# One core: the order of all work taken from a list scheduler over five engines, and the high part of each weight block rounded on GpSimd

## The chip, the cores and the metric

One core of a Trainium2 chip runs the kernel. The metric is the time of one execution in microseconds (us) on the device, the median of several runs. Five engines work side by side, each through its own queue in order: TensorE (PE, with its weight loads PEld), VectorE (DVE), ScalarE (ACT), GpSimd (POOL) and SyncE (SP), which here only issues DMA transfers. PSUM, where matmuls put their results, has eight banks of 128x512 fp32.

## The reference

```python
def phi(x):                       # x scaled by 64**-0.25
    h = einsum('bhsd,md->bhsm', x, omega) - sum(x * x, -1) / 2
    return exp(h - max(h, -1)) / sqrt(m)
q_p, k_p = phi(q_s), phi(k_s)     # 8 batches, 8 heads, 576 positions, 128 features
kv  = einsum('bhsm,bhsd->bhmd', k_p, v)
z   = sum(k_p, axis=2)
out = einsum('bhsm,bhmd->bhsd', q_p, kv) / (einsum('bhsm,bhm->bhs', q_p, z) + 1e-6)
x   = out as 4608 tokens x 512
h   = x @ w_in                    # 512 x 2048, float64 weights
result = (h * sigmoid(h)) @ w_out # 2048 x 512, float64 weights
```

## The kernel before

The attention is done in 32 windows, one for each pair of heads of a batch; four windows give the 512 channels of one batch's tokens. A window n goes through a chain over all engines. SP loads its transposed rows (`rawk`, `rawq`), its natural rows (`nat`) and `vt`. PE projects k and q (L136, eight matmuls into two banks) and the ninth, mixed chunk (L181, "mid", one bank). DVE takes the maxima (L159, L187) and forms the shift `nb` (L152, L153); for the first eight windows (`DIRECT`) ACT applies the exponential straight from the bank (L167, L191), later DVE subtracts (L171, L193) and ACT does one exponential over the tile (L199). POOL adds up k's features (L209 to L214), PE spreads the sum to all rows (L220), ACT copies it (`zb`), DVE forms the denominators (L265 to L269), POOL divides (L272), PE transposes q's nine chunks in three groups (L283), ACT copies each (L284), PE multiplies with the turned kv (L293), and ACT and DVE split the result into a high and a low part (`xh`, `xl`, L304, L305).

The MLP runs in 9 x 16 = 144 steps (t, f): t is a block of 512 tokens (the ninth holds the last 64 tokens of each batch), f a block of 128 of the 2048 columns. All operands are split in a high and a low fp32r part, so that a step has 12 matmuls of stage 1 (L409) into a bank `ph`, two Silu activations on ACT (L413, L414), a subtraction on DVE (`gl`, L415), and, two steps later (`LAG`), 12 matmuls of stage 2 (L425) into the four accumulators `po`. Two banks serve `ph`, so stage 1 of step i+2 needs `gl` of step i to be done. The weights come as float64. A block of 128x512 is put together from its words: ACT L371, DVE L372, L373 and L376, then ACT rounds the high part (L377) and POOL subtracts (L378). There are 32 blocks, all prepared during the first 16 steps; those of `w_out` also go to DRAM (`wo_d`) and are read again for t > 0.

The order is written by hand: each piece of work is put into one list with a key (`POS` and `PPOS` give a window's keys, 8 units are one step, a window takes 32) and the list is sorted by key; the framework then lays the instructions out, engine by engine. Windows 0 to 3 and parts of window 4 come before the first step. From step 2 on attention has two banks (`ps_a`), in turn; before that it uses up to eight.

Of the kernel before, what the change touches and what calls it, by code (L numbers as in the profile page):

```python
# [18 lines left out]
P = 128  # L19
# [32 lines left out]
PPOS = {
    "loadk": 1, "loadq": 1.1, "loadv": 1.2, "sqk": 6, "sqq": 6.1,
    "z": 0, "kv": 1, "zcopy": 1.2, "den": 2.2, "norm": 5, "kvturn": 2,
    "projk": 0.1, "evack": 0.3, "midk": 0.2, "mevack": 0.4, "turn": 12.2,
    "projq": 0.5, "evacq": 6, "midq": 0.6, "mevacq": 6.1, "expk": 1.5, "expq": 8, "sums": 9,
    "num": 14,
}
# [3 lines left out]
def attention_mlp(ctx: ExitStack, tc: tile.TileContext, qT, kT, qn, kn, v, om_in, w_in, w_out, out):  # L62
# [4 lines left out]
    xs = ctx.enter_context(tc.tile_pool(name="xs", bufs=2))  # L67
    mlp = ctx.enter_context(tc.tile_pool(name="mlp", bufs=2))
    att = ctx.enter_context(tc.tile_pool(name="att", bufs=1))
    dram = ctx.enter_context(tc.tile_pool(name="dram", bufs=1, space=DRAM))  # L70
    ps_acc = ctx.enter_context(tc.tile_pool(name="ps_acc", bufs=4, space=PSUM))
    ps_h = ctx.enter_context(tc.tile_pool(name="ps_h", bufs=2, space=PSUM))
    ps_att = ctx.enter_context(tc.tile_pool(name="ps_att", bufs=2, space=PSUM))
# [6 lines left out]
    oms = const.tile([P, M], F32, tag="oms", name="oms")  # L80

    def warm(count):
        ps = ps_att.tile([P, 512], F32, tag="att", name="ps_warm")
        for _ in range(count):
            nc.tensor.matmul(ps[:, :P], ones, ones, start=True, stop=True)

    wide = [8]
    rr = [0]

    def bank():  # L90
        if wide[0]:
            rr[0] += 1
            i = rr[0] % wide[0]
            if i < 4:
                return ps_acc.tile([P, 512], F32, tag="acc", name="ps_w")
            if i >= 6:
                return ps_h.tile([P, 512], F32, tag="h", name="ps_w2")
        return ps_att.tile([P, 512], F32, tag="att", name="ps_a")

    raws, nats, sqs, hs, mxs, nbs, banks, mids, vts = {}, {}, {}, {}, {}, {}, {}, {}, {}  # L100
# [4 lines left out]
    def load(n, who):  # L105
        b, p = divmod(n, NPAIR)
        srcT, srcn = (kT, kn) if who == "k" else (qT, qn)
        raw = att.tile([P, S + P], F32, tag=f"raw{who}", name=f"raw{who}", bufs=2)
        nc.sync.dma_start(raw, srcT[b, p])
        if n == 0 and who == "k":  # L110
            nc.scalar.dma_start(omr, om_in)
        nat = att.tile([P, NC, D], F32, tag="nat", name="nat", bufs=2)
        nc.sync.dma_start(nat, srcn[b, p])
        raws[n, who], nats[n, who] = raw, nat

    def load_v(n):
        b, p = divmod(n, NPAIR)
        vt = att.tile([P, NC + 1, D], F32, tag="v", name="vt", bufs=2)
        nc.sync.dma_start(vt, v[b, p])
        vts[n] = vt  # L120

    def squares(n, who):
        nat = nats.pop((n, who))
        nc.scalar.activation(nat, nat, AF.Square, scale=SCALE * 0.5**0.5)  # L124
        s = att.tile([P, 10], F32, tag=f"sq{who}", name="sq", bufs=2)
        nc.vector.tensor_reduce(s[:, :NC], nat, AX.X, ALU.add)
        sqs[n, who] = s

    def project(n, who):
        raw = raws[n, who]  # L130
        pair = [bank(), bank()]
# [7 lines left out]
        banks[n, who] = pair
        hs[n, who] = att.tile([P, NC, M], F32, tag=f"h{who}", name=f"h{who}", bufs=2)  # L140
        mxs[n, who] = att.tile([P, 10], F32, tag=f"mx{who}", name="mx")
        nbs[n, who] = att.tile([P, 10], F32, tag=f"nb{who}", name="nb")
# [7 lines left out]
    def shift(n, who, part):  # L150
        m, s, nb = part(mxs[n, who]), part(sqs[n, who]), part(nbs[n, who])
        nc.vector.tensor_tensor(nb, m, s, ALU.subtract)  # L152
        nc.vector.scalar_tensor_tensor(nb, nb, -1.0, s, ALU.mult, ALU.subtract)  # L153

    def evacuate(n, who):
        h, m, nb = hs[n, who], mxs[n, who], nbs[n, who]
        pair = banks.pop((n, who))
        for j in range(2):
            nc.vector.tensor_reduce(  # L159
                m[:, 5 * j : 5 * j + 4], pair[j].rearrange("p (c m) -> p c m", m=M), AX.X, ALU.max  # L160
            )
        shift(n, who, sides)
        for j in range(2):
            if n < DIRECT:
                for i in range(4):
                    c = 5 * j + i
                    nc.scalar.activation(  # L167
                        h[:, c], pair[j][:, i * M : (i + 1) * M], AF.Exp, bias=nb[:, c : c + 1]
                    )
                continue  # L170
            nc.vector.tensor_tensor(  # L171
                h[:, 5 * j : 5 * j + 4],
                pair[j].rearrange("p (c m) -> p c m", m=M),
                nb[:, 5 * j : 5 * j + 4].unsqueeze(2).broadcast_to([P, 4, M]),
                ALU.add,
            )

    def project_mid(n, who):
        raw = raws.pop((n, who))
        ps = bank()  # L180
        nc.tensor.matmul(ps[:, :M], raw[:, S:], oms, start=True, stop=True)  # L181
        mids[n, who] = ps

    def evacuate_mid(n, who):
        h, m, nb = hs[n, who], mxs.pop((n, who)), nbs[n, who]
        ps = mids.pop((n, who))
        nc.vector.tensor_reduce(m[:, 4:5], ps[:, :M], AX.X, ALU.max)  # L187
        mxs[n, who] = m
        shift(n, who, middle)
        if n < DIRECT:  # L190
            nc.scalar.activation(h[:, MID], ps[:, :M], AF.Exp, bias=nb[:, 4:5])  # L191
        else:
            nc.vector.tensor_scalar(h[:, MID], ps[:, :M], nb[:, 4:5], None, ALU.add)  # L193
        del mxs[n, who], nbs[n, who], sqs[n, who]

    def expo(n, who):
        if n < DIRECT:
            return
        nc.scalar.activation(hs[n, who], hs[n, who], AF.Exp)  # L199

    ess, zbs, kvs, ens, kts = {}, {}, {}, {}, {}
# [46 lines left out]
    def kv_alone(n):  # L248
        kv(n)
        kt_copy(n)  # L250
# [285 lines left out]
```

## Time and profile before

| | |
|---|---|
| runs | 1109.34 us median of 3 (1109.12 to 1111.86) |
| profiled execution | 1111.65 us, span of the core 1109.8 us |
| busy share of the span | PE 96%, PEld 76%, ACT 53%, DVE 50%, POOL 21% |
| granted TensorE clock | 0.977 of full speed over the span |
| HBM | 138.48 MB read, 19.92 MB written, 143 GB/s |

The span is the time from the first to the last instruction; the execution's own time is 1.85 us longer. A busy share is an average over stages that have different limits: the first 80 us are attention alone, steps 0 to 15 do attention, MLP and the preparation of weights together, steps 16 to about 112 attention and MLP, and the rest the MLP alone.

### The profile page before, as it was taken

The page shows a single profiled execution, that of the slowest core. Times are in us where ns is not written, and L with a number is a line of the kernel's source. Part 1 is how long each engine was busy: PE and PEld are TensorE (multiplying, and loading weights), DVE is VectorE, ACT ScalarE, POOL GpSimd, SP SyncE. Part 2 cuts the span into 40 slices and gives each one's busy share as a digit, 9 for nine tenths or more (in the row PEclk, how much of TensorE's full clock was granted, in tenths as well). Part 3 has the DMA queues.
Part 4 walks back from the last instruction along what each step waited for, and adds up shares of the span by engine and source line. Part 5 has one row for each costly group of instructions (what it writes and reads, how often), then busy time and mean ns, then how long its engine had stood idle before and what let it go on. Part 6 is the DMA issues. An engine that isn't in the chain of part 4 may idle for free.

```text
span 1109.8 us, 16167 instructions
## 1 busy us (share of the span) xinstructions
PE 1066.0 (96%) x5900; PEld 841.2 (76%) x5900; DVE 558.6 (50%) x1125; ACT 584.2 (53%) x1105; POOL 229.5 (21%) x295
## 2 busy tenths in 40 slices
PE   7679898999999999999999999999999999999998
PEld 6447676777778777777777777777777788888886
DVE  6887987745555555455554555455544431111111
ACT  6759677565555555655556555655555542112221
POOL 3544544411111111111111111111111110000000
PEclk7769999999999999999999999999999999999999
DMA  7556666454444344444345444434343226233322
GB/s 264 173 169 213 228 207 226 166 167 128 131 131 162 112 136 138 145 145 132 126 130 164 138 138 128 164 126 135 116 139 113 69 79 203 98 103 118 116 95 76
DMA packets 64223, 159.46 MB, mean 144 GB/s; under 512 B 15376, under 2 KB 15504, under 8 KB 64144
## 3 DMA queue, kind: packets, MB, share of 16 engines
q1 hardware_dynamic: 63680, 157.84, 44.1%
q8 instruction: 47, 0.77, 0.3%
q10 hardware_dynamic: 464, 0.59, 0.2%
q14 instruction: 32, 0.26, 0.1%
HBM read 138.48 MB, written 19.92 MB: 143 GB/s over the span
## 4 chain that ended last, share of the span: by engine, by line
PE 80%; DVE 7%; ACT 6%; issue 2%; POOL 2%; DMA 2%; SPq 0%; ACTq 0%; DVEq 0%; POOLq 0%
PE ph L409 32%; PE po L425 31%; PE ps_a L136 6%; PE ps_a L283 3%; PE ps_a L238 2%; PE ps_a L293 2%; DMA out<-ot 1%; PE ps_a L220 1%; PE ps_a L181 1%; DVE prod L265 1%; ACT L413 1%; ACT L199 1%; DVE w L373 1%; DVE mx L159 1%; DVE w L372 1%
## 5 line engine op out<-in xcount | busy, mean ns | idle before, releaser
L425 PE MATMUL po<-wo,gh 128*128 128x512 f32 x1152 | 379.3, 406 | 0.0
L413 ACT ACTIVATE gh<-ph 128x512 fp32r<-128x512 f32 x144 | 86.2, 599 | 329.2 <-PE ph L409 328.6
L415 DVE TENSOR_TENSOR gl<-ph,gh 128x512 fp32r<-128x512 f32 x144 | 99.0, 687 | 283.1 <-ACT ph L414 283.1
L425 PEld LDWEIGHTS po<-wo,gh 128*128 128x128 f32 x1152 | 205.5, 188 | 40.3 <-ACT hk L167 0.4
L409 PE MATMUL ph<-xh,wh 128*128 128x512 f32 x576 | 233.7, 406 | 0.0
L409 PE MATMUL ph<-xl,wh 128*128 128x512 f32 x576 | 226.7, 394 | 0.0
L409 PE MATMUL ph<-xh,wl 128*128 128x512 f32 x576 | 226.4, 393 | 0.0
L425 PE MATMUL po<-wo,gl 128*128 128x512 f32 x576 | 226.1, 393 | 0.0
L272 POOL TENSOR_TENSOR hq<-hq,rd 128x384 f32<-128x384 f32 x96 | 81.4, 877 | 404.1 <-DVE rd L269 352.8
L159 DVE TENSOR_REDUCE mx<-ps_a 128x4 f32<-128x512 f32 x112 | 73.1, 686 | 119.9 <-PE ps_a L136 119.2
L409 PEld LDWEIGHTS ph<-xh,wh 128*128 128x128 f32 x576 | 108.4, 188 | 26.0 <-issue 1.6
L409 PEld LDWEIGHTS ph<-xh,wl 128*128 128x128 f32 x576 | 108.6, 188 | 23.4
L409 PEld LDWEIGHTS ph<-xl,wh 128*128 128x128 f32 x576 | 108.6, 189 | 23.3
L425 PEld LDWEIGHTS po<-wo,gl 128*128 128x128 f32 x576 | 108.2, 188 | 22.4
L413 ACT ACT_TABLE_LOAD x54 | 69.3, 1283 | 40.1 <-PE ph L409 39.4
L209 POOL TENSOR_TENSOR t<-hk 128x256 f32<-128x256 f32 x64 | 46.2, 737 | 210.6 <-ACT hk L199 180.1
L414 ACT ACTIVATE ph<-ph 128x512 f32<-128x512 f32 x144 | 85.4, 593 | 0.0
L199 ACT ACT_TABLE_LOAD x47 | 60.3, 1283 | 33.8 <-DVE hq L193 33.4
L265 DVE TENSOR_TENSOR prod<-hq,zb 128x512 f32<-128x512 f32 (+1 forms) x96 | 49.0, 563 | 35.0 <-ACT zb L229 34.9
L283 PE MATMUL ps_a<-ident,hq 128*128 128x128 f32 x258 | 43.4, 281 | 10.9 <-ACT hk L191 6.6
L124 ACT ACTIVATE nat<-nat 128x576 f32<-128x576 f32 x64 | 44.8, 702 | 15.1 <-DMA nat<-kn 12.5
L283 PEld LDWEIGHTS ps_a<-ident,hq 128*128 128x128 f32 x258 | 31.1, 142 | 26.8 <-issue 7.6
(96 smaller groups left out, 1190.0 us busy)
## 6 DMA issues: line engine op xcount, KB each, us to landing
wo<-wo_d SPq DMA_DIRECT2D x128, 512.0 KB, 3.4
rawk<-kT SPq DMA_DIRECT2D x32, 352.0 KB, 3.0
rawq<-qT SPq DMA_DIRECT2D x32, 352.0 KB, 3.0
vt<-v SPq DMA_DIRECT2D x32, 320.0 KB, 3.0
nat<-kn SPq DMA_DIRECT2D x32, 288.0 KB, 3.0
nat<-qn SPq DMA_DIRECT2D x32, 288.0 KB, 3.1
wraw<-w_in SPq DMA_DIRECT2D x16, 512.0 KB, 3.9
wraw<-w_out SPq DMA_DIRECT2D x16, 512.0 KB, 4.3
```

Of the source, the lines that this page charges most:

```text
L136: nc.tensor.matmul(pair[j][:, i * M : (i + 1) * M], raw[r, o : o + P], oms[r], start=True, stop=True)
L159: nc.vector.tensor_reduce(m[:, 5 * j : 5 * j + 4], pair[j].rearrange("p (c m) -> p c m", m=M), AX.X, ALU.max)
L199: nc.scalar.activation(hs[n, who], hs[n, who], AF.Exp)
L209: nc.gpsimd.tensor_tensor(t[:, j], e[:, 5 * j : 5 * j + 2], e[:, 5 * j + 2 : 5 * j + 4], ALU.add)
L265: nc.vector.tensor_tensor(prod[:, c, :M], e[:, c], zb[:, j].unsqueeze(1).broadcast_to([P, hi - lo, M]), ALU.mult)
L272: nc.gpsimd.tensor_tensor(e[:, c], e[:, c], rd[:, c].unsqueeze(2).broadcast_to([P, 3, M]), ALU.mult)
L283: nc.tensor.transpose(ps[:, i * P : (i + 1) * P], e[:, 3 * g + i], ident)
L409: nc.tensor.matmul(ph, w[:, k, :], x, start=k == 0 and n == 0, stop=k == NK - 1 and n == 2)
L413: nc.scalar.activation(gh, ph, AF.Silu)
L414: nc.scalar.activation(ph, ph, AF.Silu)
L415: nc.vector.tensor_tensor(gl, ph, gh.bitcast(F32), ALU.subtract)
L425: nc.tensor.matmul(accs[t][j], g[:, js], w, start=f == 0 and n == 0, stop=f == NF - 1 and n == 2)
```

## The change

Every piece of work becomes a unit of a plan, with its engine, a duration written in by hand, a key, what it must follow, and which buffers it takes and frees. A loop takes, over and over, the unit that can start first (with keys deciding within 0.25 us) and so makes one list, in which the units are then recorded. The framework lays out the instructions from that list. Four more things change. The high part of a weight block is rounded by POOL in place of ACT. The word buffer `w32` has three slots in place of two. A block of `w_out` is read back from DRAM at t = 0 as well (16 more reads), through a ring of three in place of four. In windows 0 to 3 the shift is formed in one piece, and x is split in 512+64 columns in place of 288+288.

```diff
+RINGS = {
+    "acc": 4, "h": 2, "att": 2,
...
+    "en": 2, "den": 2, "rd": 2, "wraw": 3, "w32": 3, "wre": 2, "wo": 3, "wp": 2, "gh": 3, "gl": 3, "ot": 2,
+}
+START_MLP = 62.0
+STEP = 7.56
+SLOW = 8.2
+PRO = 11.0
+SWITCH = 1.3
+STAY = 8.0
+HANDOFF = {"PE": 0.3, "ACT": 0.15, "DVE": 0.15, "POOL": 0.2, "SP": 0.2}
+CALM = 0.5
...
+                p = min((p for p in pick if p[3] <= least + 0.25), key=lambda p: p[2:])
+                if best is None or p[3] < best[3]:
+                    best = p
...
+            free_at[e] = t + dur
...
-        nc.scalar.copy(hi, w)
-        nc.gpsimd.tensor_tensor(lo, w, hi.bitcast(F32), ALU.subtract)
...
+    def weight_high(i):
+        nc.gpsimd.tensor_copy(parts_of(i)[0], T["w", i])
+
+    def weight_low(i):
+        hi, lo = parts_of(i)
+        nc.gpsimd.tensor_tensor(lo, T["w", i], hi.bitcast(F32), ALU.subtract)
+
+    def keep_weight(f):
+        nc.sync.dma_start(wo_d[f].bitcast(F32), T.pop(("wp", f)).bitcast(F32))
+
+    def get_weight(t, f):
+        T["wo", t, f] = wo = new("wo", [P, 2, DMODEL], F32R)
+        nc.sync.dma_start(wo.bitcast(F32), wo_d[f].bitcast(F32))
...
+        add(("wh",) + i, "POOL", 0.9, key - 1, lambda: weight_high(i), after=[("wd",) + i + (2,)], alloc=list(more))
+        add(("wlo",) + i, "POOL", 1.05, key, lambda: weight_low(i), after=[("wh",) + i], free=[("w32",) + i])
...
-    for _, f in sorted(queue, key=lambda e: e[0]):
-        f()
+    for u in plan.run():
+        u["fn"](*[bank(p) for p in u["pools"]])
```

The number of instructions stays nearly the same: PE has the same matmuls (eight 64x512 and eight 64x64 products take the place of sixteen 64x288), DVE 1111 rows with its two branches counted against 1127, POOL 32 CASTs more, ACT 32 CASTs fewer and 120 table loads against 108, SP 16 loads of `wo` more.

The first place is PE's queue in steps 6 and 7, where the transposes of window 5 (L283, now L381) meet the mixed chunk of window 6's k (L181, now L269); L409 and L495 are stage 1, L425 and L513 stage 2. Before:

```order
L425 MATMUL po_1100<-wo,gh 128x512
L181 MATMUL ps_a<-oms,rawk 128x128
L425 MATMUL po_1100<-wo,gh 128x512
L425 MATMUL po_1100<-wo,gl 128x512
L425 MATMUL po_1101<-wo,gh 128x512 x2
L283 MATMUL ps_a<-ident,hq 128x128 x3
L425 MATMUL po_1101<-wo,gl 128x512
L409 MATMUL ph<-xh_346,wh_1203 128x512
L283 MATMUL ps_a<-ident,hq 128x128 x6
```

Now:

```order
L381 MATMUL ps_att<-ident,hq 128x128 x3
L495 MATMUL ps_h<-xh_730,wh_1172 128x512
L495 MATMUL ps_h<-xl_731,wh_1172 128x512
L495 MATMUL ps_h<-xh_730,wl_1173 128x512
L269 MATMUL ps_att<-oms,rawk 128x128
L495 MATMUL ps_h<-xh_954,wh_1172 128x512
L381 MATMUL ps_att<-ident,hq 128x128 x3
L495 MATMUL ps_h<-xl_955,wh_1172 128x512
L495 MATMUL ps_h<-xh_954,wl_1173 128x512
L513 MATMUL ps_acc<-wo,gh 128x512 x2
L513 MATMUL ps_acc<-wo,gl 128x512
L381 MATMUL ps_att<-ident,hq 128x128 x3
```

The three groups of transposes are spread out, the mixed chunk stands behind the first of them, and the group that takes the mixed chunk's bank (the second before, the third now) is still only six MLP matmuls and one group away from it.

The second place is DVE's queue around the maximum of that same mixed chunk (L187, now L276), with the word operations of weight blocks (L372, L373, L376; now L456, L458, L462) and the shift (L152, L153; now L282, L283). Before:

```order
L373 SCALAR_TENSOR_TENSOR w32_1351<-wre_1352,w32_1351 128x512
L372 TENSOR_SCALAR w32_1377<-wraw_1375 128x512
L376 SCALAR_TENSOR_TENSOR w32_1351<-wraw_1349,w32_1351 128x512
L373 SCALAR_TENSOR_TENSOR w32_1377<-wre_1378,w32_1377 128x512
L376 SCALAR_TENSOR_TENSOR w32_1377<-wraw_1375,w32_1377 128x512
L187 TENSOR_REDUCE mx_1307<-ps_a_1346 128x1
L152 TENSOR_TENSOR nb_1308<-mx_1307,sq_1032 128x1
L153 SCALAR_TENSOR_TENSOR nb_1308<-nb_1308,sq_1032 128x1
```

Now:

```order
L458 SCALAR_TENSOR_TENSOR w32_1409<-wre_1418,w32_1409 128x512
L276 TENSOR_REDUCE mxk_1342<-ps_att_1415 128x1
L462 SCALAR_TENSOR_TENSOR w32_1409<-wraw_1329,w32_1409 128x512
L282 TENSOR_TENSOR nbk_1343<-mxk_1342,sqk_907 128x1
L458 SCALAR_TENSOR_TENSOR w32_1463<-wre_1477,w32_1463 128x512
L283 SCALAR_TENSOR_TENSOR nbk_1343<-nbk_1343,sqk_907 128x1
```

Before, the word operations stand ahead of the maximum; now two of them stand between the maximum and the shift's two halves.

The third place is POOL's queue at the fourth and fifth weight blocks (L378 before; L476 and L480 now), between the sums of k (L209 to L214, now L318 to L323) and the division (L272, now L375). Before:

```order
L378 TENSOR_TENSOR wl_802<-w_805,wh_801 128x512
L378 TENSOR_TENSOR wo<-w_846,wo 128x512
L209 TENSOR_TENSOR t<-hk 128x256 x2
L211 TENSOR_TENSOR es<-t 128x256
L214 TENSOR_TENSOR es<-es,hk 64x128 x2
L272 TENSOR_TENSOR hq<-hq,rd 128x384 x3
```

Now:

```order
L476 CAST wh_759<-w_693 128x512
L480 TENSOR_TENSOR wl_760<-w_693,wh_759 128x512
L476 CAST wp<-w_552 128x512
L318 TENSOR_TENSOR t<-hk 128x256
L480 TENSOR_TENSOR wp<-w_552,wp 128x512
L318 TENSOR_TENSOR t<-hk 128x256
L320 TENSOR_TENSOR es<-t 128x256
L476 CAST wh_939<-w_914 128x512
L480 TENSOR_TENSOR wl_940<-w_914,wh_939 128x512
L323 TENSOR_TENSOR es<-es,hk 64x128 x2
L375 TENSOR_TENSOR hq<-hq,rd 128x384 x3
```

Each block now has two instructions on POOL, and they stand between those of the attention.

## Rows read from the trace of the kernel before

**Rows 1.** Busy time by engine in stretches of the span, TensorE's granted clock, DMA.
```profile
core 0: us, PE busy (x) PEld busy (x) DVE busy (x) ACT busy (x) POOL busy (x), PEclk, DMA share, GB/s
97.50:198.40 100.90, 87.68 (x467) 66.83 (x467) 83.69 (x141) 75.29 (x162) 47.12 (x42) 0.97 0.63 210
198.40:247.60 49.20, 47.44 (x281) 36.96 (x279) 29.30 (x62) 29.94 (x50) 12.60 (x16) 1.00 0.55 176
247.60:1099.00 851.40, 849.30 (x4665) 677.67 (x4664) 368.42 (x765) 409.60 (x698) 122.53 (x179) 1.00 0.40 127
```
**Rows 2.** Timeline of PE: first matmul of steps 3 and 14; the kernel's last.
```profile
97.51 0.50 PE L409 MATMUL ph<-xh,wh 128*128 128x512 f32 x1
...
198.37 0.39 PE L409 MATMUL ph<-xh,wh 128*128 128x512 f32 x1
...
1104.98 0.39 PE L425 MATMUL po<-wo,gl 128*128 128x512 f32 x1
```
**Rows 3.** Who PE waited for, 97.5 to 198.4: total us, times, longest.
```profile
PE ps_a L283 <- ACT hk L191: 6.6, 2, 3.4
PE ps_a L220 <- DVE xl L305: 2.7, 2, 1.3
PE ps_a L181 <- ACT hk L167: 2.2, 2, 2.0
PE ps_a L181 <- ACT hq L167: 1.7, 1, 1.7
```
**Rows 4.** The same view from 198.4 to the end.
```profile
PE ps_a L220 <- DVE xl L305: 2.9, 4, 1.3
```
**Rows 5.** Timeline of DVE, ACT and PE at one of the waits of rows 3.
```profile
128.76 1.22 DVE L373 SCALAR_TENSOR_TENSOR w<-wre,w 128x512 uint32<-128x512 uint32 x1
130.01 1.09 DVE L376 SCALAR_TENSOR_TENSOR w<-wraw,w 128x512 uint32<-128x512 uint32 x1
131.03 0.28 DVE L187 TENSOR_REDUCE mx<-ps_a 128x1 f32<-128x128 f32 x1
...
132.47 0.37 ACT L191 ACTIVATE hk<-ps_a,nb 128x128 f32<-128x128 f32 x1 [2.92 <-DVE nb L153]
...
132.98 0.78 PE L283 MATMUL ps_a<-ident,hq 128*128 128x128 f32 x5 [3.24 <-ACT hk L191]
```
**Rows 6.** Stretches up to the ends of gl of steps 1 and 12, as rows 1.
```profile
0.00:91.40 91.40, 69.14 (x431) 50.43 (x432) 71.96 (x150) 61.81 (x178) 43.24 (x54) 0.76 0.64 204
0.00:193.30 193.30, 157.81 (x909) 117.48 (x910) 154.28 (x287) 140.59 (x349) 91.40 (x97) 0.87 0.64 210
```
**Rows 7.** DVE by line, 0 to 193.3: busy us, mean ns, idle before.
```profile
L376 DVE SCALAR_TENSOR_TENSOR w<-wraw,w 128x512 uint32<-128x512 uint32 x29 | 23.4, 818 | 0.1
L372 DVE TENSOR_SCALAR w<-wraw 128x512 uint32<-128x512 uint32 x30 | 23.0, 775 | 12.8 <-POOL wo L378 7.7 <-POOL wl L378 5.1
L373 DVE SCALAR_TENSOR_TENSOR w<-wre,w 128x512 uint32<-128x512 uint32 x29 | 21.4, 747 | 0.2
L152 DVE TENSOR_TENSOR nb<-mx,sq 128x8 f32<-128x8 f32 x16 | 6.8, 424 | 0.0
```
**Rows 8.** Single lines of DVE over the whole span: duration ns, min/median/max.
```profile
L372 DVE TENSOR_SCALAR w<-wraw x32: 413/462/1568, 27.0 to 199.7; 128x512 uint32<-128x512 uint32 x32
L376 DVE SCALAR_TENSOR_TENSOR w<-wraw,w x32: 673/683/1533, 32.6 to 203.4; 128x512 uint32<-128x512 uint32 x32
L152 DVE TENSOR_TENSOR nb<-mx,sq x128: 142/160/1259, 8.7 to 893.3; 128x8 f32<-128x8 f32 x64, 128x1 f32<-128x1 f32 x64
```
**Rows 9.** POOL by line, 0 to 193.3, as rows 7.
```profile
L378 POOL TENSOR_TENSOR wl<-w,wh 128x512 fp32r<-128x512 f32 x16 | 21.5, 1342 | 9.3 <-ACT wh L377 8.9
L272 POOL TENSOR_TENSOR hq<-hq,rd 128x384 f32<-128x384 f32 x21 | 21.0, 1025 | 15.4 <-DVE rd L269 14.0 <-DVE nb L153 0.9 <-DVE nb L152 0.4
L203 POOL MEMSET prod<- 128x1161 f32 x1 | 1.1, 1072 | 0.0
```
**Rows 10.** ACT by line, 0 to 193.3, as rows 7: one group.
```profile
L413 ACT ACT_TABLE_LOAD x7 | 9.0, 1283 | 0.1
```
**Rows 11.** DMA issues of the weights read again: KB each, us to landing.
```profile
wo<-wo_d SPq DMA_DIRECT2D x128, 512.0 KB, 3.4
```

More of the change, by code (lines that the diff above doesn't have):

```diff
@@ L103, in omega @@
         nc.scalar.mul(oms, omr, SCALE)
[L105 to L114, printed above, removed]
@@ L116, in load_v @@
-    def load_v(n):
[L117 to L123, printed above, removed]
-        nc.scalar.activation(nat, nat, AF.Square, scale=SCALE * 0.5**0.5)
[L125 to L131, printed above, removed]
+    T = {}
@@ L139, in project @@
[L139 to L142, printed above, removed]
+                nc.tensor.matmul(ps[:, i * M : (i + 1) * M], raw[r, o : o + P], oms[r], start=True, stop=True)
+        T["p", n, who, 0], T["p", n, who, 1] = a, b
+        T["h", n, who] = new(f"h{who}", [P, NC, M])
+        T["mx", n, who] = new(f"mx{who}", [P, 10])
@@ L144, in sides, with shift, every @@
+    def shift(n, who, part):
+        m, s, nb = (part(T[a, n, who]) for a in ("mx", "sq", "nb"))
+        nc.vector.tensor_tensor(nb, m, s, ALU.subtract)
+        nc.vector.scalar_tensor_tensor(nb, nb, -1.0, s, ALU.mult, ALU.subtract)
+    def every(a):
+        return a[:, :NC]
     def sides(a):
@@ L148, in middle @@
         return a[:, 4:5]
[L150 to L192, printed above, removed]
+    def expo(n, who, j):
+        h, nb, ps = T["h", n, who], T["nb", n, who], T.pop(("p", n, who, j))
+        for i in range(1 if j == 2 else 4):
+            c = 4 if j == 2 else 5 * j + i
+            nc.scalar.activation(h[:, c], ps[:, i * M : (i + 1) * M], AF.Exp, bias=nb[:, c : c + 1])
@@ L463, in attention_mlp, with at, bk @@
-    for n in range(LEAD, NWIN):
-        queue += window(n, POS, SPACE * (n - LEAD))
-    for f in range(NF):
-        put(8 * (f - AHEAD_IN) + 4.5, weights_in, f)
-    for i in range(NF * (B + 1)):
-        put(8 * (i - AHEAD_OUT) + 3.5, weights_out, *divmod(i, NF))
+    plan = Plan()
+    add = plan.add
+    def at(n, off, steady):
+        if n < LEAD:
+            return PRO * n + off
+        return clock(4 * (n - LEAD - 1) + steady / 8)
+    def bk(name, j=0):
+        return ("bank", name, j)
@@ new lines, in attention_mlp @@
+    last = None
+    for f in range(NF):
+        key = clock(f)
+        weight(("in", f), key - 4, w_in[f], last)
+        last = ("in", f)
+        weight(("out", f), clock(f + LAG) - 3, w_out[f], last,
+               more=[("wp", ("wp", f))])
+        last = ("out", f)
+        add(("keep", f), "SP", 0.42, clock(f + LAG) + 4, lambda f=f: keep_weight(f), after=[("wlo", "out", f)], lat=2.1,
+            free=[("wp", f)])
+    steps = [(t, f) for t in range(B + 1) for f in range(NF)]
+    total = len(steps)
```

703 lines of the change are left out of this document (461 added, 242 removed).

## The prediction

> **What bounds the kernel now.** I read the stretches first, since the busy shares of the whole span average over stages. From 247.6 us to 1099 TensorE works 849.3 of 851.4 us at clock 1.00 [rows 1]: nothing that another engine does there can move the end, and the change leaves PE the same matmuls. So the end moves only by what is gained or lost ahead of about step 20. From step 3 to step 14, 97.5 to 198.4, PE is busy 87.68 of 100.90 us, so 13.2 are idle at clock 0.97 [rows 1]. From there to 247.6 only 1.8 us are idle [rows 1].
>
> Next, who PE waited for. Between 97.5 and 198.4 the four entries sum to 13.2 us, all of the idle time, and every one is a wait for a bank of attention (`ps_a`): 6.6 for the transposes, whose bank still holds k's mixed chunk that ACT has not read; 2.7 for the sum of k (L220), whose bank's last content DVE has not yet split; 3.9 for the mixed chunk's matmul [rows 3]. After 198.4 L220 waits another 2.9 [rows 4]. The timeline shows the costliest wait from inside: the maximum of the mixed chunk starts on DVE at 131.03 behind word operations of 1.22 and 1.09 us, ACT's exponential at 132.47 waited 2.92 us for DVE, and the transposes start at 132.98 after 3.24 us of idle PE [rows 5].
>
> Last, DVE, the engine behind those waits, and its neighbour POOL. Up to 193.3, the end of step 12's `gl` on which step 14 depends, DVE is busy 154.28 us and so idle 39.0 [rows 6]; step 14's first matmul stands at 198.37, 5.1 later [rows 2]. DVE's busy time holds more than the operations need: L372 takes 413 ns at its shortest and 1568 at its longest [rows 8], 775 in the mean up to 193.3 [rows 7].
>
> **The change, part by part.** *The order.* The same count of matmuls stands ahead of steps 3, 8, 14 and 20 in both orders (283, 446, 658, 879; now 878), so no work is moved across these places on PE, and what counts is when the banks come free. Three terms.
>
> (a) Up to step 3. It starts at 97.51 [rows 2], and needs `gl` of step 1, which ends at 91.4 with DVE busy 71.96 us and idle 19.4 [rows 6]. The new order has 153 DVE instructions ahead of that `gl` where 148 were: the words of twelve weight blocks in place of eight, and fewer attention pieces. The words of four blocks at their minima, 0.41 + 0.67 + 0.67 each, are 7.0 [rows 8] with L373 taken as L376; the rest of the exchange I put at 2, by counting, and the locks (below) at 2. So DVE is busy 83. Before, the idle 19.4 were mostly waits for transfers and banks; with more work at hand I take 14 to be left. 83 + 14 = 97 for `gl` would be 5 late; but the `gl` of step 1 no longer stands as far ahead of step 3's place on PE, where 283 matmuls must be done in either order by then at the same clock. I take 0, with bounds of -5 (the idle time shrinks by 5 more) and +5.4 (all of it shows).
>
> (b) Steps 3 to 14. The wait of L220 goes: PE work between the last user of its bank and L220 was 2.6 us and is 5.7 to 6.9 in the new order, against a longest wait of 1.3 [rows 3]: -2.7. The transposes wait little less. In the second place of the order the distance from the mixed chunk to the group that takes its bank is 1.9 to 2.5 us of PE work where it was 1.6 to 1.9, and of DVE's chain the word operations that stood ahead of the maximum now stand between it and the two halves of the shift: the chain is no shorter by them. On ACT the mixed chunk's exponential stands between the Silu activations of a step in some windows, which costs table loads of 1.28 us [rows 10]. I take -2.0 of 6.6. The mixed chunk's matmul has less distance than before in one of its two kinds (6.6 and 5.6 us, against 9.5 and 5.7): 3.9 stay. Sum -4.7; bounds -13.2 (all idle time gone) and 0.
>
> (c) After step 14. L220's distance rises from 2.6 to 3.3 or 4.0 us; its four waits average 0.7 [rows 4]: -2.5 of 2.9.
>
> *The cast on POOL.* On ACT it frees 32 instructions, but ACT is idle 53 us of 193 [rows 6] and is waited for only through DVE [rows 5], so the gain there is nothing beyond (b), and twelve more table loads of 1.28 us give back 15.4. POOL has no such cast in the trace. Bounds: a memset is 1072 ns for 1161 columns, so 0.47 for 512; the subtraction of the same size, with two inputs, is 1342 [rows 9]. The division is 1025 for 384 columns, at times held up [rows 9]; the cast has one input and 512. I take 0.95, nearest that row: 30 casts up to step 14 are 28.5 us on an engine that is busy 91.4 of 193.3 [rows 6], so POOL has the room. What it costs is DVE's time. DVE and POOL hold each other up in this trace: L372 is 775 against 413 in 30 instructions, L376 818 against 673 in 29, L373 747 against the same in 29, L152 424 against a median of 160 in 16 [rows 7, 8], and L153 like it, which makes 10.9 + 4.2 + 2.1 + 4.2 + 3.7 = 25 us for POOL's 91.4. In proportion, 28.5 us more of POOL cost DVE 0.27 x 28.5 = 7.8; by the bounds 3.8 and 11.0.
>
> [...]
>
> *The third word slot, the whole shift and the wider split.* L372 waits 12.8 us for POOL to free a word slot [rows 7]; with three slots in place of two and POOL's chain per block longer by the cast, I expect about 9 of it to go as idle DVE time. Up to `gl` of step 12 DVE has 273 instructions where 286 were: sixteen shifts fewer and the splits merged, against the words moved in from steps 13 to 15, about -2 us of durations. So DVE would be busy 154.3 - 2 + 7.8 = 160, and with 30 us idle in place of 39 this `gl` ends at 190, before it is needed. If the idle time stays, see the third rival.
>
> *The order of DMA.* `wo` of t = 0 now goes to DRAM and back, 3.4 us each way [rows 11], two to three steps (100.9 / 11 = 9.2 us each) ahead of stage 2: hidden. Uncovered, the first would cost PE up to 3.4. Sixteen more reads of 512 KB are queued on SP behind slots that come free late, and the inputs of the next window behind them; DMA is busy 0.63 there [rows 1], so I add nothing. PE's finer alternation of attention and MLP adds nothing either, since matmuls follow one another either way at their own durations.
>
> Sum: 0 - 4.7 - 2.5 = -7.2. Against the profiled execution's own 1111.65 that is 1104.4; the median of the runs is 1109.34, 2.3 below the profiled execution, which puts the prediction at **1102**.
>
> **The rivals.** *Larger gain.* The scheduler knows the banks, so PE's waits may go altogether, and the start may be five earlier: -13.2 - 3.9 - 5 = -22, 1087. For it: all idle time of PE is bank waits [rows 3]. Against it: the distances above, and the durations in the plan know nothing of locks.
>
> *No change.* The waits only change place: k's and q's shifts wait behind word operations as before, kv's matmul stands only 0.5 to 2.7 us of PE work behind q's transposes, and the table loads split the Silu pair that frees `ph`. -7 is then used up, 1109. For it: the second place of the order.
>
> *Slower.* DVE with its locks becomes the bound of steps 5 to 14. If its idle time stays at 39, `gl` of step 12 ends at 160 + 39 = 199, and step 14 at 199 + 5.1 = 204, +6 to +7 against 198.37; 1116. It decides from the point where DVE's idle time up to that `gl` stays above about 33 us; with the upper price of the cast it is 3 more, 1119. For it: POOL's share rises from 0.47 to 0.62 just where L372 is already held to twice its minimum. Against it: 12.8 of the 39 are the word slots [rows 7].
> [...]
>
> **How the numbers follow.** Forecast (-7, 1102) 0.45; larger gain 0.15; no change 0.20; slower 0.20. A difference under 0.3%, 3.3 us, can't be told from none. The likeliest case's own range is 1097 to 1106. For eight in ten the range reaches from the larger gain to the slower case, without their outer ends: 1088 to 1116. Faster 0.45 + 0.15 = 0.60, same 0.20, slower 0.20.
>
> **What would show it.** Right: the waits of L327 (L220 before) gone between steps 3 and 14; those of the transposes (L381) still 4 to 5 us; step 14's first matmul near 193 and the stretch behind step 20 unchanged; POOL's cast near 0.95 us, and L456 (L372 before) longer in the mean than 775 ns. Wrong: a cast of 1.3 us or more, a `gl` of step 12 later than 197, a stage 1 that waits for `ph`, stage 2 waiting for `wo`, or a DVE idle time that did not shrink.

## The result, and the profile after

The changed kernel takes 1100.12 us in the median of four runs (1097.0 to 1101.4), against 1109.44 for the kernel before measured beside it; the ratio is 0.9899, with a 95% interval of 0.988 to 0.9918. So it is 9.3 us faster. The number lies two us from the forecast. The place does not: the forecast put the gain ahead of step 20, where in the profiled execution nothing is gained, and nothing behind it, where all of it is.

The profiled execution of the changed kernel took 1101.40 us, its span is 1099.3. TensorE's timeline shows the first matmuls of steps 3, 14 and 20 and the last of all; they answer to [rows 2].

```profile
109.29 0.39 PE L495 MATMUL ps_h<-xh,wh 128*128 128x512 f32 x1
...
201.21 0.39 PE L495 MATMUL ps_h<-xh,wh 128*128 128x512 f32 x1
...
249.97 0.39 PE L495 MATMUL ps_h<-xh,wh 128*128 128x512 f32 x1
...
1094.37 0.39 PE L513 MATMUL ps_acc<-wo,gl 128*128 128x512 f32 x1
```

Step 3 comes 11.8 us later than before (97.51); steps 3 to 14 take 91.92 in place of 100.86, 8.9 less; steps 14 to 20 take 48.76 in place of 49.2, 0.5 less; and from step 20 (247.6 before) to the last matmul it is 844.40 in place of 857.4, which is 13.0 less. The sum is -10.6 for the last matmul, of which the last stretch alone is more than the whole.

The stretches of the changed kernel, with the columns of [rows 1]: steps 3 to 14, and steps 20 to 112, the part with attention; then steps 20 to 112 of the kernel before, which were only a part of a row there.

```profile
109.30:201.20 91.90, 85.05 (x466) 64.47 (x465) 79.55 (x128) 72.64 (x142) 57.87 (x57) 1.00 0.77 263
250.00:915.10 665.10, 664.89 (x3902) 530.48 (x3901) 351.93 (x733) 370.43 (x626) 122.73 (x179) 1.00 0.41 134
```
```profile
247.60:925.70 678.10, 676.00 (x3901) 534.10 (x3900) 346.41 (x733) 370.45 (x626) 122.53 (x179) 1.00 0.41 131
```

The reader is to see three things. Between steps 3 and 14 PE's idle time is 6.85 us where it was 13.2, and the granted clock is 1.00 where it was 0.97. In steps 20 to 112 the same 3901 or 3902 matmuls at the same clock of 1.00 have 11.1 us less of busy time: a busy time that shrinks without fewer matmuls held waits. And the idle time that could be read off before in that stretch was only 2.1 us.

Where the waits were, the groups of TensorE in steps 32 to 112 of both kernels say: q's projection (L136, now L262), the transposes (L283, now L381) and the sum of k (L220, now L327).

```profile
L283 PE MATMUL ps_a<-ident,hq 128*128 128x128 f32 x180 | 29.8, 275 | 0.0
L136 PE MATMUL ps_a<-oms,rawq 64*128 64x128 f32 x304 | 29.4, 285 | 0.0
L136 PE MATMUL ps_a<-oms,rawk 64*128 64x128 f32 x304 | 22.1, 285 | 0.0
L220 PE MATMUL ps_a<-es,ones 128*128 128x256 f32 x40 | 12.2, 387 | 2.1 <-DVE xl L305 2.1
```
```profile
L381 PE MATMUL ps_att<-ident,hq 128*128 128x128 f32 x180 | 26.2, 273 | 0.0
L262 PE MATMUL ps_att<-oms,rawq 64*128 64x128 f32 x304 | 23.9, 285 | 0.2 <-ACT en L385 0.2
L262 PE MATMUL ps_att<-oms,rawk 64*128 64x128 f32 x304 | 22.1, 285 | 0.0
L327 PE MATMUL ps_att<-es,ones 128*128 128x256 f32 x40 | 11.9, 378 | 0.0
```

The projections of q and of k are the same work, in 19 windows here. Before, q's was busy 29.4 us and k's 22.1; now they are 23.9 and 22.1. One window of before, from 288 to 293 us, in the timeline of DVE, PE's weight loads (PEld), PE and ACT:

```profile
288.01 0.35 DVE L193 TENSOR_SCALAR hk<-ps_a,nb 128x128 f32<-128x128 f32 x1
...
288.05 0.48 PE L425 MATMUL po<-wo,gh 128*128 128x512 f32 x1
...
288.48 0.31 PEld L283 LDWEIGHTS ps_a<-ident,hq 128*128 128x128 f32 x3 [0.27 <-issue]
...
290.12 1.17 ACT L199 ACTIVATE hk<-hk 128x1152 f32<-128x1152 f32 x1
291.19 0.84 ACT L284 COPY en<-ps_a 128x384 f32<-128x384 f32 x2
...
291.84 1.21 PEld L136 LDWEIGHTS ps_a<-oms,rawq 64*128 64x128 f32 x16 [0.37 <-ACT en L284]
291.84 1.40 PE L136 MATMUL ps_a<-oms,rawq 64*128 64x128 f32 x16
293.17 0.50 PE L409 MATMUL ph<-xh,wh 128*128 128x512 f32 x1
```

The second group of transposes needs the bank of k's mixed chunk, which DVE (L193) reads until 288.36; its weight load comes at 288.48, 0.27 us after the one before it ended, and that gap is all that can be seen, since the matmul ahead of it, at 288.05 with a modelled 0.48 us, covers it on PE's own row. (The view names no releaser for the gap; that it is a wait, which goes when the group stands later, is shown by e2 below.) Then ACT does its exponential and only afterwards copies the second and third group of transposes out (291.19 to 292.03). Q's projection takes those two banks and starts at 291.84, with the second still held; the weight load's row names that copy, and from the projection's first matmul to the next piece of work it is 1.33 us. In the same window of the changed kernel the copies end ahead of the projection:

```profile
294.26 0.84 ACT L385 COPY en<-ps_att 128x384 f32<-128x384 f32 x2
...
295.23 1.16 PE L262 MATMUL ps_att<-oms,rawq 64*128 64x128 f32 x16
```

It takes 1.09 us to the next piece at 296.32. A group of four steps, one window, takes 29.42 us before and 28.99 to 29.05 after; at a change of batch (steps 32 to 36, and every sixteen steps from there) it takes 30.2 to 31.7 before and 29.4 to 29.7 after.

Of the terms ahead of step 20, DVE's stretches up to the ends of `gl` of steps 1 and 12 answer to [rows 6], its groups to [rows 7], and the cast can now be read (0 to 195.7):

```profile
0.00:108.40 108.40, 75.17 (x463) 53.34 (x464) 83.88 (x154) 67.53 (x192) 63.80 (x76) 0.76 0.69 232
0.00:195.70 195.70, 156.38 (x902) 114.54 (x902) 158.82 (x274) 139.71 (x331) 117.17 (x128) 0.87 0.74 250
```
```profile
L462 DVE SCALAR_TENSOR_TENSOR w<-wraw,w 128x512 uint32<-128x512 uint32 x30 | 25.9, 880 | 0.1
L458 DVE SCALAR_TENSOR_TENSOR w<-wre,w 128x512 uint32<-128x512 uint32 x30 | 25.4, 857 | 0.4 <-ACT wre L442 0.4
L456 DVE TENSOR_SCALAR w<-wraw 128x512 uint32<-128x512 uint32 x32 | 23.0, 721 | 10.4 <-POOL wp L480 4.1 <-POOL wl L480 3.5 <-DMA wraw<-w_out 2.2
...
L476 POOL CAST wh<-w 128x512 fp32r<-128x512 f32 x15 | 12.2, 816 | 13.7 <-DVE w L462 7.5 <-DVE nbq L282 4.6 <-DVE nbk L283 1.4
L476 POOL CAST wp<-w 128x512 fp32r<-128x512 f32 x15 | 11.4, 761 | 11.7 <-DVE w L462 10.9 <-DVE nbk L282 0.6
```

DVE is busy 83.9 and 158.8 us, as worked out (83 and 160). But it is idle 24.5 and 36.9 us, where 14 and 30 were taken.

### The profile page after: what moved, and what is told of

Read it like the earlier page. It is cut to its first block, busy times and chain, and to the rows that moved or that the text cites. A ratio compares the mean times of both kernels' runs of the same rounds, so it can differ in the third digit from the quotient of the medians.

```text
span 1099.3 us, 16192 instructions
## 1 busy us (share of the span) xinstructions
PE 1053.1 (96%) x5900; PEld 834.5 (76%) x5900; DVE 566.4 (52%) x1109; ACT 583.1 (53%) x1085; POOL 255.5 (23%) x327
## 4 chain that ended last, share of the span: by engine, by line
PE 86%; DVE 5%; DMA 3%; ACT 3%; POOL 1%; issue 1%; SPq 0%; ACTq 0%; DVEq 0%; POOLq 0%
PE ps_acc L513 35%; PE ps_h L495 34%; PE ps_att L262 5%; PE ps_att L343 3%; PE ps_att L381 3%; PE ps_att L399 2%; DMA wraw<-w_out 1%; DMA nat<-qn 1%; PE ps_att L327 1%; PE ps_att L269 1%; DVE w L458 1%; ACT hq L298 1%; DVE w L462 1%; POOL hq L375 1%; DVE den L369 1%
## 5 line engine op out<-in xcount | busy, mean ns | idle before, releaser
L513 PE MATMUL ps_acc<-wo,gh 128*128 128x512 f32 x1152 | 369.9, 402 | 0.0
L513 PEld LDWEIGHTS ps_acc<-wo,gh 128*128 128x128 f32 x1152 | 207.1, 189 | 43.7
L495 PE MATMUL ps_h<-xh,wh 128*128 128x512 f32 x576 | 235.0, 409 | 0.3 <-ACT xh L413 0.3
L495 PE MATMUL ps_h<-xh,wl 128*128 128x512 f32 x576 | 226.7, 394 | 0.0
L495 PE MATMUL ps_h<-xl,wh 128*128 128x512 f32 x576 | 225.9, 392 | 0.0
L513 PE MATMUL ps_acc<-wo,gl 128*128 128x512 f32 x576 | 225.8, 392 | 0.0
L375 POOL TENSOR_TENSOR hq<-hq,rd 128x384 f32<-128x384 f32 x96 | 81.7, 879 | 421.4 <-DVE rd L370 396.5
L495 PEld LDWEIGHTS ps_h<-xh,wh 128*128 128x128 f32 x576 | 108.1, 188 | 24.7 <-issue 0.8
L513 PEld LDWEIGHTS ps_acc<-wo,gl 128*128 128x128 f32 x576 | 108.1, 188 | 24.2 <-issue 0.8
L495 PEld LDWEIGHTS ps_h<-xh,wl 128*128 128x128 f32 x576 | 108.1, 188 | 24.1
L495 PEld LDWEIGHTS ps_h<-xl,wh 128*128 128x128 f32 x576 | 108.5, 188 | 22.3 <-DVE xl L418 0.4
L318 POOL TENSOR_TENSOR t<-hk 128x256 f32<-128x256 f32 x64 | 48.8, 780 | 183.2 <-ACT hk L312 170.1
L381 PE MATMUL ps_att<-ident,hq 128*128 128x128 f32 x261 | 41.1, 284 | 7.9 <-POOL wp L476 2.4
```

The lines of the kernel that those rows point to most:

```text
L318: nc.gpsimd.tensor_tensor(t[:, j], e[:, 5 * j : 5 * j + 2], e[:, 5 * j + 2 : 5 * j + 4], ALU.add)
L375: nc.gpsimd.tensor_tensor(e[:, c], e[:, c], rd[:, c].unsqueeze(2).broadcast_to([P, 3, M]), ALU.mult)
L381: nc.tensor.transpose(ps[:, i * P : (i + 1) * P], T["h", n, "q"][:, 3 * g + i], ident)
L495: nc.tensor.matmul(ph, w[:, k, :], x, start=k == 0 and n == 0, stop=k == NK - 1 and n == 2)
L513: nc.tensor.matmul(T["po", t][j], g[:, js], w, start=f == 0 and n == 0, stop=f == NF - 1 and n == 2)
```

## The experiments

Two theories stood against each other on the steady part. A: short waits for banks inside each window, hidden under the modelled ends of matmuls. B: the finer alternation of the pieces, or another engine. On the start: the cast (C) or the order alone (D).

**One number in the order by hand (e1).** From window 9 on, q's projection three matmuls later:

```diff
+LATE = dict(POS, projq=18)        # 17 in POS
-        queue += window(n, POS, SPACE * (n - LEAD))
+        queue += window(n, POS if n < 9 else LATE, SPACE * (n - LEAD))
```

> The kernel before, with one number changed from window 9 on: the projection of q stands one stage-1 block (three matmuls, 0.69 us) later on TensorE; nothing else moves. Theory A (short bank waits inside the steady steps, under the modelled ends of the matmuls): q's projection takes 1.09 us in place of 1.33 as in the changed kernel, 22 windows by 0.25 and some 0.6 more at each of five changes of batch: 8 to 9 us faster, and a group of four steps takes 29.18 in place of 29.42. Theory B (the scheduler's order is faster because attention and MLP alternate in other pieces, or because of the engines around TensorE): the pieces stay the same, so nothing: within 1 us.

Measured: 1103.31 us, ratio 0.9949 (0.9927 to 0.997). An ordinary group of four steps, one away from the changes of batch, takes 29.19, as A said to a hundredth. The gain of 6 us is less than 8 to 9, because the changes of batch kept most of their extra time (below). The projection in this kernel:

```profile
289.40 1.16 PE L136 MATMUL ps_a<-oms,rawq 64*128 64x128 f32 x16
290.50 0.50 PE L409 MATMUL ph<-xh,wh 128*128 128x512 f32 x1
```

It takes 1.10 us to the next piece. The orders of DVE and ACT are unchanged, so B has nothing to explain this with.

**The transposes alone (e2).** The second group two matmuls later, directly ahead of the third:

```diff
-            for g in range(3):
-                add("turn", turn, n, g, d=0.8 * g)
+            for g in range(3):
+                add("turn", turn, n, g, d=0.8 * g if not g else pos.get("gap", 0.8) + 0.8 * (g - 1))
...
+LATE = dict(POS, gap=1.0)
```

> The kernel before, from window 9 on the second group of q's transposes stands two MLP matmuls later, directly ahead of the third, which stays. Theory A: the 0.235 us for which that group waits for its bank (held by the mixed chunk of k until DVE has read it) go in 23 windows: 5.4 us faster, a group of four steps 29.19. Theory B: one piece less per window, a few hundredths of a us each: under 1 us.

Measured: 1108.36, ratio 0.9993 (0.9977 to 1.0009); four steps at 29.45. That missed A's number. Working out, for each kind of matmul, the time from its start to the next start, summed over an ordinary window (us), shows where it went:

```
                before   e1_q   e2_turn  e3_both  changed
q's projection   1.330   1.091   1.466    1.092    1.092
transposes       0.765   0.765   0.819    0.818    0.820
stage 2         12.091  12.096  11.857   11.855   11.665
stage 1         11.386  11.392  11.456   11.403   11.503
all             29.42   29.19   29.45    29.02    29.01
```

The wait did go (0.23 us less in stage 2, ahead of the group), and the projection, now reached earlier, waits longer for the same two copies: 0.14 more there and 0.07 in the matmul ahead of it. The 0.05 in the transposes stand in the next run and in the changed kernel too, where nothing waits, and so go with six of them in a row. (Kinds that are not in the table are the same in all five, but for k's chunks, 0.08 longer in the changed kernel.) So of 0.23 us taken away 0.21 are waited for again at the next stall.

**Both (e3).** LATE holds projq=18 and gap=1.0.

> Both moves together in the kernel before. Theory A: they add up, 13 to 14 us faster than before, four steps at 28.95 to 29.0, which is the changed kernel's 28.99; the whole is then faster than the changed kernel (1100.1), since the start of before is 2.4 us ahead of it: about 1096. Theory B: under 2 us.

Measured: 1101.56, ratio 0.9928 (0.9907 to 0.9949); four steps at 29.02. The ordinary window is thus that of the changed kernel, from two keys moved by hand. The total missed by some 5 us: the five groups at a change of batch took 29.65 to 31.06, those of the changed kernel 29.35 to 29.66. PE waits there for the bank of k's sum, which holds a result that DVE has not yet split behind ACT's copies of the accumulators:

```profile
L220 PE MATMUL ps_a<-es,ones 128*128 128x256 f32 x40 | 12.2, 387 | 3.2 <-DVE xl L305 3.1
```

**The sum of k later too (e5).** LATE has also z=1.5 and zcopy=2.0, so that L220 stands behind six matmuls of stage 1; in the changed kernel it is six in 17 windows and three in 6.

> The kernel before with both moves of the last run and, from window 9 on as well, the sum of k (L220) two stage-1 blocks (six matmuls) later, where the changed kernel has it; the copy of its result follows it. Theory A: what the last run still loses at the changes of batch is that sum's wait for its bank behind the copies of the finished accumulators on ACT (0.01 to 1.41 us, 3.8 in all over the five): it goes, the five boundary groups come down from 29.65 to 31.06 to about 29.4 as in the changed kernel, ordinary groups stay at 29.02; 3.5 to 4 us faster than the last run, about 1097.5. Rival: the copies of the accumulators themselves hold the next thing on ACT up and the wait moves to stage 2 or the products: under 1 us faster.

Measured: 1096.78, ratio 0.9878 (0.986 to 0.9895). The five boundary groups take 29.53 or 29.54, ordinary ones 29.01; the same group of L220 has no wait left:

```profile
L220 PE MATMUL ps_a<-es,ones 128*128 128x256 f32 x40 | 11.9, 380 | 0.0
```

From step 20 to step 112 this kernel takes 665.8 us, the changed one 665.1, the one before 678.1. So three moves give all that the scheduler gave in the steady part. A holds.

**The same from window 6 on (e6).**

> The same three moves from window 6 on in place of 9, so in steps 8 to 20 too, where weights are still prepared. Theory A: the sum's waits there (part of 2.7 + 2.9 us) and three more windows at 0.45 us go: 2 to 4 us faster than the last run, about 1094 to 1096, faster than both kernels. Rival: where DVE and POOL still prepare weights the chain over the engines sets the pace and a later sum only delays the division: no gain, or up to 3 us slower than the last run.

Measured: 1097.70, ratio 0.9886 (0.9871 to 0.9901), no different from the last; from step 3 to the last matmul the two profiled executions take 993.9 and 993.8 us. The rival was nearer: where weights are still prepared, these moves give nothing.

**The cast alone (e4).** In the kernel before:

```diff
-        nc.scalar.copy(hi, w)
+        nc.gpsimd.tensor_copy(hi, w)
```

> The kernel before with the cast of the weights' high part on GpSimd and nothing else changed in the code. Theory C (the cast loads GpSimd, which is waited for at the start, and blocks DVE): step 3 comes 3 to 8 us later, DVE's word operations are longer, and the whole is 3 to 8 us slower. Theory D (the cast is free, the later start of the changed kernel comes from its order alone): step 3 and the whole within 1.5 us of before.

Measured: 1116.51, ratio 1.0061 (1.0038 to 1.0083), 7 us slower. Step 14 comes at 205.5 where it was 198.4, with as many matmuls ahead of it; from step 20 on nothing changes. Step 3 comes at 100.1, with 18 matmuls fewer ahead than before, since with the cast on another engine the framework also lays some pieces of the first steps out otherwise. So the 7 us are the edit's, and not in every part the cast's. Two views show a wait that [rows 3] does not have:

```profile
PE ph L409 <- DVE gl L415: 7.7, 3, 4.1
PE ps_a L181 <- ACT hk L167: 3.7, 2, 3.1
```
```profile
L372 DVE TENSOR_SCALAR w<-wraw 128x512 uint32<-128x512 uint32 x30 | 19.5, 649 | 14.7 <-POOL wo L378 9.8 <-POOL wl L378 4.9
```

Stage 1 waits for its own banks, behind `gl` on DVE: 4.1 us up to step 3's first matmul at 100.05, and 3.6 in two waits behind it. DVE's group up to 193.3 shows that L372 is shorter in the mean than before (649 against 775 ns); L376 and L373 are 817 and 771 against 818 and 747, so it is not longer word operations, the other half of C. L372 waits longer for a word slot, which GpSimd's subtraction frees (14.7 against 12.8 us). In two of the three waits, among them the longest, DVE stands at just that, with `gl` behind it in its queue:

```profile
98.74 0.66 DVE L372 TENSOR_SCALAR w<-wraw 128x512 uint32<-128x512 uint32 x1 [3.08 <-POOL wl L378]
99.32 0.68 DVE L415 TENSOR_TENSOR gl<-ph,gh 128x512 fp32r<-128x512 f32 x1
```

The other of the two is 2.15 us long, ahead of a `gl` at 151.64, with two word operations and two maxima in between. By these rows C was right that GpSimd holds the start up, by way of the word slot.

**The cast back on ACT (e7)** in the changed kernel, with its plan as it is:

```diff
-        nc.gpsimd.tensor_copy(parts_of(i)[0], T["w", i])
+        nc.scalar.copy(parts_of(i)[0], T["w", i])
```

> The changed kernel with its plan as it is, and only the cast of the high part issued on ACT again. Theory C (the cast costs what it cost in the kernel before, 7 us, through GpSimd's queue and DVE's word operations): step 3 two to four us earlier, step 14 four to seven, the whole 4 to 7 us faster than the changed kernel, 1093 to 1096. Theory D (the plan has counted on it and hides it): within 1.5 us, or slower by up to 3 since ACT's activations wait behind the casts.

Measured: 1099.82, ratio 0.9904 (0.9887 to 0.992), the same as the changed kernel. Step 14 comes 4.7 us earlier (196.5), of which 2.7 stand at step 3 already, and steps 14 to 20 give 3.0 back, 51.8 us in place of 48.8. The waits from 190 to 245 us say for what:

```profile
PE ps_h L495 <- POOL wl L480: 3.1, 2, 2.7
PE ps_att L327 <- POOL es L323: 2.8, 1, 2.8
```

Stage 1 waits for the last weight blocks at GpSimd's subtraction, though GpSimd no longer rounds them, and PE's sum of k (L327) for GpSimd's (`es`). The changed kernel has neither wait in that stretch. PE's order is not quite the same here either: step 16 stands behind 28 matmuls fewer (steps 3, 14 and 20 behind as many).

**A third word slot (e8)** in the kernel before (bufs=3 for `w32`).

> The kernel before with three slots for the words of the weights in place of two. Theory E (the prediction's step): of the 12.8 us that L372 waits for GpSimd some 9 go, DVE is ahead of time at step 14, and the steps up to there, which wait for DVE's results in part, come 2 to 5 us earlier. Rival: the words only wait one operation later, since the subtraction on GpSimd comes no sooner: within 1.5 us of before.

Measured: 1111.64, ratio 1.0016 (1.0001 to 1.0032). No gain, and 2.1 us more in the median, a little outside the rival's 1.5. L372's idle time is what it was, and now waits in part for the raw weights:

```profile
L372 DVE TENSOR_SCALAR w<-wraw 128x512 uint32<-128x512 uint32 x30 | 22.7, 775 | 12.3 <-DMA wraw<-w_out 4.8 <-POOL wo L378 3.8 <-DMA wraw<-w_in 2.0
```

**The reserve ahead of PE's units (e9).** The changed kernel with CALM = 0.

> The changed kernel with the plan's extra 0.5 us ahead of TensorE's units set to 0 (CALM = 0): from about step 13 on q's projection stands two stage-1 matmuls (0.46 us) earlier in each window, and a few pieces near step 14 move; the rest is the same. Theory A: the two copies that free q's banks end 0.13 us ahead of the projection now, so it starts with its second bank still held and its pairs of matmuls fall out of step: an ordinary group of four steps takes 29.2 to 29.4 in place of 28.99, 22 windows by 0.2 to 0.4 make the whole 4 to 9 us slower than the changed kernel, 1104 to 1109. Theory B: the count of pieces is the same, so within 1 us.

Measured: 1098.55, ratio 0.9894 (0.9875 to 0.9914), the same as the changed kernel. It tells nothing of A: only pieces of steps 13 to 16 differ in the order, q's projection stands nine matmuls into its step in both (seven at a change of batch, in both), and windows take 28.99. The move that the expectation counted on is not there.

**A third slot for the natural rows (e10)** (`nat`), planned anew, in the changed kernel. It was tried since in the chain that leads to step 3 of the changed kernel two loads of these rows stand on the path, each issued as DVE ends a sum over older rows (`sqk` or `sqq`) and so frees their slot; one of them, start, us, what:

```profile
53.05 0.77 DVE sqk L254
...
53.83 4.20 DMA nat<-qn
...
58.11 0.69 ACT nat L250
...
58.83 0.76 DVE sqq L254
59.58 1.27 DVE den L369
```

> The changed kernel with three slots for the natural rows of q and k in place of two, planned anew with that (8 weight blocks stand ahead of the gl of step 0 in place of 10). Theory I (step 3 is late because the chain there waits for those loads, 4.2 and 5.8 us, behind a slot that DVE frees late): step 3 comes 4 to 8 us earlier than the changed kernel's 109.3, the whole 3 to 6 us faster than it, 1094 to 1097. Rival S (the start is bound by the work of DVE and GpSimd, which take the weights in early): step 3 may move, but step 14 and the whole stay within 2 us of the changed kernel.

Measured: 1093.68, ratio 0.9853 (0.983 to 0.9877), the fastest of all, 6 us below the changed kernel and 16 below the one before. Step 3 comes at 99.55, 9.7 us earlier than in the changed kernel, step 14 at 191.1, 10.1 earlier, and step 20 at 242.5, 7.4 earlier. Theory I gave the time; that the slot alone did it is not shown, since the plan with that slot also takes the first weight blocks later, and the two were not told apart.

**That kernel with the cast on ACT (e11).**

> The last run's kernel (the changed kernel planned with three slots for the natural rows, 1093.7) with the cast of the high part on ACT, plan as it is. Theory C (GpSimd's cast is a load that the plan only hides behind the waits for inputs): with those waits gone it shows, 3 to 6 us faster, about 1089. Theory D (what ends steps 14 to 16 is the chain that prepares the last weight blocks, and the cast is a link of it on either engine): within 2 us of 1093.7.

Measured: 1098.15, ratio 0.9898 (0.9884 to 0.9913), 4.5 us slower. Neither theory had this: the cast is better on GpSimd here, as far as the edit goes, which moves some pieces on PE too (step 14 stands behind eight matmuls more). PE waits more for ACT's exponentials, in whose queue the casts now stand (100 to 250 us):

```profile
PE ps_att L262 <- ACT hk L298: 3.5, 2, 2.9
PE ps_h L495 <- POOL wl L480: 2.8, 2, 2.4
```

**That slot in the order by hand (e12)** (bufs=3 for `nat`, on the kernel with three moves).

> The best run in the order by hand (all three moves from window 9 on, 1096.8) with three slots for the natural rows. TensorE's order is the same, only loads move forward on SP. Theory I (those loads hold the start up in either order): step 3 comes 2 to 5 us earlier and the whole with it, 1092 to 1095. Rival (in the order by hand the loads come in time; the start there waits for GpSimd's divisions): within 1.5 us of 1096.8.

Measured: 1100.95, ratio 0.9931 (0.991 to 0.9951), 4 us slower than without. PE's order is the same, and so is the steady part (665.9 us); step 3 came at 97.92 against 94.03, a difference that profiles of one and the same order show as well (last section). Only the loads' order on SP moved, and how it costs the 4 us was not found out. The gain of e10 does not carry over to this order.

## Why the prediction was right in its number and wrong in its reason

The number was luck: four errors nearly cancel (the sum stands at the end of this section).

*What bounds the kernel.* This step failed: "nothing that another engine does there can move the end". It rested on 849.3 busy of 851.4 us [rows 1]. A matmul of 512 columns starts 0.23 us after the one before (201.21 and 201.44 in the changed kernel) and stands in the trace with 0.39 us, so a wait of up to 0.16 us hides wholly in the overlap, and of a longer one as much; a row such as "1.40 us for 16" holds waits within itself. All 13.0 us of the gain behind step 20 came from there (worked out as in the table above). Seventeen ordinary groups give 7.0: in each 0.24 us from q's projection, which waits for a bank behind ACT's exponential, and 0.17 net from the second group of transposes, once the projection is out of the way. Five groups at a change of batch give 6.3: in each 0.44 from q's projection, 0.1 to 1.5 from k's sum, and the rest from the transposes and their neighbours; the last group gives 0.2 back. e1, e3 and e5 show the three of them. In steps 20 to 112 PE's busy share was 0.997 and rose to 1.000, while that of the weight loads went from 534.10 / 678.1 = 0.788 to 530.48 / 665.1 = 0.798; the first seemed to leave 2.1 us to gain, where 13.0 were.

*Term (a), step 3, taken as 0 with bounds of -5 and +5.4.* Measured +11.8, outside the bounds. DVE's busy time was right to 1 us; its idle time did not shrink to 14 but grew to 24.5. The plan begins step 0 at 41.8 us, where it was 78.9, and still reaches step 3 later. Inputs that wait for a slot, behind sums that DVE does late, stand on the chain; with a third slot, and the plan that it gives, step 3 came 9.7 us earlier (e10). The cast is not the larger part: with it back on ACT step 3 came 2.7 earlier (e7), no more than profiles of one order differ by. That loads could become late had been costed at nothing ("the inputs of the next window behind them").

*Term (b), steps 3 to 14, -4.7.* Measured -8.9, within its bounds: 6.4 of idle time and 2.6 of busy time, which the sum had not counted. The second goes with the clock, 0.97 to 1.00: with before's order in this stretch PE is busy 87.7 us at a clock of 0.97 [rows 1] and 88.9 at 0.95 (e5, 94.0 to 195.0), and 87.6, 89.0 and 89.7 at 0.97, 0.95 and 0.93 (e3, e1, e2). How much of it is time is open, since these stretches differ by 1 us only (100.9 and 101.0; 100.9, 100.8 and 101.7). L220's waits fell from 2.7 to 1.0, the mixed chunk's 3.9 are gone, which had been said to stay, and the transposes' are 3.2 in place of 6.6 (-2.0 had been taken):

```profile
PE ps_att L381 <- POOL wp L476: 2.4, 1, 2.4
PE ps_att L351 <- DVE xl L418: 2.0, 1, 2.0
PE ps_att L327 <- ACT hq L298: 1.0, 2, 0.7
```

*Term (c), -2.5.* Measured -0.5.

*The cast, 0.95 us.* It takes 0.79 in the mean and 0.60 to 0.61 at the shortest. As for what the prediction calls locks, no run shows a lock; what the trace of the kernel before shows is an L372 that is longer only beside GpSimd's instructions. Of the 32 of L372 the ten with no GpSimd instruction at the same time take 413 to 428 ns, the other 22 take 413 to 1568, 956 in the mean. Two of them, one beside the division and one behind it:

```profile
25.34 2.40 POOL L272 TENSOR_TENSOR hq<-hq,rd 128x384 f32<-128x384 f32 x3 [4.94 <-DVE rd L269]
...
27.00 1.02 DVE L372 TENSOR_SCALAR w<-wraw 128x512 uint32<-128x512 uint32 x1
...
28.03 0.42 DVE L372 TENSOR_SCALAR w<-wraw 128x512 uint32<-128x512 uint32 x1
```

With the casts on GpSimd L456 did not become longer (721 ns against 775), L458 and L462 did (857 and 880 against 747 and 818). In all, the word operations' busy time rose by 6.5 us (74.3 against 67.8); four instructions more make 2.2 of that by the minima, which leaves about 4 for these lines, where 7.8 were taken for all of DVE. A price in proportion to GpSimd's time is not borne out: in e4 GpSimd is busy 112.0 us up to 193.3 in place of 91.4, and the same 88 word operations take 65.3 in place of 67.8. In the order by hand the edit costs 7 us, the price of the slower rival; but the wait is for a slot and the `gl` behind it (e4), not for longer word operations. In the plan it costs nothing (e7), since the stretch behind gives back what the start would gain.

*The third word slot, some 9 of 12.8 us.* Failed: 10.4 are left, and alone it gains nothing (e8). Of the 10.4, 7.6 still wait for GpSimd's subtraction, which frees the slots whatever their number, and 2.2 for the raw weights.

*The whole shift, the wider split, `wo` by way of DRAM.* Costed at nothing or 2 us, and not tried apart. `wo` is in none of the waits of PE above.

*The signs.* Of those named for being right, step 14 near 193 (201.2), an unchanged stretch behind step 20 (-13.0) and a longer L456 (721 ns) did not come; the transposes waited 3.2 us and not 4 to 5, L327 1.0 and not 0. The cast alone came out near its number.

So errors of +11.8, -4.2, +2.0 and -13.0 against the steps nearly cancel (-3.4), and the range held the time by that.

## What to carry to other kernels

On a full TensorE, set the time from one matmul's start to the next beside that of the same work elsewhere (here q's projection beside k's): where it is longer, look for a hidden wait, whatever the busy share says, and move the piece to test it, since neighbours alone can shift such a sum a little (0.05 us in e2). What a list scheduler gives in a steady loop can be a few moves in an order by hand. Taking a stall away may give nothing until the next one on that engine has room too (in e2 0.21 of 0.23 us were waited for again), so try them together. Where a plan takes in more work early, see what it pushes back; here loads that wait for a slot stood on the chain.

## What the runs showed of the hardware

The start of one and the same order is not repeatable: up to window 9 the kernels before, e1, e2, e3 and e5 are the same, and step 3 came at 97.5, 95.7, 98.5, 95.7 and 94.0 us in their profiled executions. The granted clock of their first 40 us differed from 0.77 to 1.00, and did not go with it: the two ends of that range, before (0.78 and 0.76 in the first two stretches of 20 us) and e2 (1.00 and 1.00), have step 3 within 1 us of one another. A difference of up to 4.5 us at step 3 in single profiles is therefore no evidence, neither the 2.7 of e7 nor the 3.9 of e12. Behind step 3 these runs agree better: steps 3 to 14 take 100.8 to 101.7 us, steps 14 to 20 47.9 to 49.2. The differences that the argument rests on (11.8 and 9.7 at step 3, 8.9 up to step 14, 3.0 in e7 up to step 20) are clear of both. Sixteen 64-row pieces of a projection take 1.09 us where both banks are free at the start (at 295.23 in the changed kernel), 1.33 where the second comes 0.2 us late (at 291.84 in the kernel before), and 1.9 where, at a change of batch, it comes 0.77 late (at 350.92 in the kernel before). There the changed kernel and e5 still take 1.46, with the second bank 0.33 late: a wait of 0.37 us at each of five changes of batch is left.
